# Attention loads on 96 and 80 rows, with edges and repeated rows copied on chip

## The chip, the cores and the metric

The kernel runs on one core of one Trainium2 chip. The metric is the device time of one execution in microseconds, from the timed runs; lower is better. TensorE (PE) multiplies matrices, VectorE (DVE) and ScalarE (ACT) work element by element, GpSimd (POOL) here issues gathers and scatters by index, SyncE (SP) issues the plain DMA transfers, one after another in a fixed order.

## The reference

Sparse attention for 8 batches, 8 heads, 576 positions and 64 numbers per head, followed by a mixture of 8 experts. Heads 0 to 3 look back over the last 32 positions ("local"), heads 4 to 7 over all earlier positions of the same remainder modulo 32 ("strided").

```
scores = scale * q @ k^T
mask_local   = (rel >= 0) & (rel < 32)
mask_strided = (rel >= 0) & (pos_k % 32 == pos_q % 32)
attn = softmax(where(mask, scores, -1e9));  x = attn @ v
logits = x @ w_gate + log1p(exp(x @ w_noise)) * noise
for each token, its two best experts e, with softmax weights w:
    out += w * (relu(x @ w1[e]) @ w2[e])
```

## The kernel before

**Stages.** Attention is done in 32 units: 8 batches x 2 pairs of heads x (strided, local). A unit loads q, k and v of two heads (`loads`), transposes q and k so that the head dimension lies on partitions (`prep`), multiplies scores (`products`), takes exponentials, transposes them and multiplies by v (`item`), and stores the result to a table in DRAM (`finish`). After four units a batch is routed to experts (`route`). The expert stage (`experts`) gathers tokens by index and runs both layers of eight experts. It is by far the longer stage, and starts when the tokens of the first batches are routed.

**A local unit.** `raw` holds four neighbouring positions in each of 128 rows for two heads, 512 positions in all; the last 64 positions of k and q come apart as `kq0`. `raw` is reordered on chip into `ord` (a copy on VectorE or ScalarE, whichever is free earlier), TensorE transposes it in four pieces (L475), one copy empties the result from PSUM into `kT_l` or `qT_l`. `kq0` is transposed at L500 and emptied by two small copies. `v_l` has 96 rows for each block of 64 positions: the 32 rows before the block and the block itself. So each value row that ends a block is loaded twice, and the very first block has a load of its own.

**A strided unit.** `ks` and `qs` hold eight neighbouring positions in each of 72 rows; TensorE transposes them in two halves of four (L485). A query block looks at keys of the same remainder modulo 8; for the first 64 positions a separate operand is kept, which comes from `kq0` again. `v_s` has the values in 72 rows, `v_0` those of the first 64 positions.

**What sets the order.** Every step is a `Piece` with an engine, a duration from a cost function, what it reads and writes, and a rank. `issue_all` goes through all pieces once, at build time, and puts the one that could start earliest by these costs next on its engine; among those within 120 ns the lowest rank goes first. A piece marked "ANY" goes to VectorE or ScalarE. The result is one fixed sequence on each engine. SyncE's loads are costed by their bytes, and 600 ns of SyncE each. On the chip an engine executes its sequence in order and waits for what is not there yet. Buffers are rings: `raw` has two, `ks`, `qs` and `ord` one each, `v_l`, `v_s` and `v_0` two. A load into a ring waits until the last reader of the older content is done.

Names in the profile: L417 is every load of `loads`, L644 every store to the DRAM table `x_dram`; L475, L485 and L500 the transposes of `ord`, of `ks` and `qs`, and of `kq0` (`kq`); L538 the scores; L565 the row maximum `mx`; L569 and L571 exponentials `ex`; L579 the transposes of `ex` into `aT`; L598 the product with v; L262 and L263 copies on ScalarE, L265 and L266 those on VectorE; L1000 and L1064 the expert layers; L871 and L874 loads of expert weights (`wraw`).

Of the kernel before, what the change touches and what calls it, by code (L numbers as in the profile page):

```python
# [9 lines left out]
F32 = mybir.dt.float32  # L10
# [12 lines left out]
def kernel(  # L23
# [24 lines left out]
    G = S // NJ  # L48
    scale = 1.0 / math.sqrt(D)
# [49 lines left out]
    dist = consts.tile([QB, 2, G], I32, name="dist")  # L99
# [27 lines left out]
    TR = E * REG // 128  # L127
# [10 lines left out]
    qT_s = keep.tile([128, NBL, QB], F32, name="qT_s")  # L138
    v_l = [keep.tile([KW, 2, NBL, D + 1], F32, name=f"v_l{i}") for i in range(2)]
    v_s = [keep.tile([G, 2, NJ, D + 1], F32, name=f"v_s{i}") for i in range(2)]  # L140
# [14 lines left out]
    tinit = consts.tile([128, TR // 4, 3], I32, name="tinit")  # L155
# [100 lines left out]
    def dma(fn, nbytes, rank, eng="SP", **kw):  # L256
        return Piece(eng, 600 if eng == "SP" else GAP, fn, rank, lat=nbytes, **kw)
# [151 lines left out]
    def loads(u, rank):  # L409
# [10 lines left out]

        for key, src in (("k", k), ("q", q)):
            if local:

                put(key, R["raw"].new(), [(lambda t: t.rearrange("p h j d -> p h (j d)"), src, base,
                                           [[4 * D, 128], [S * D, 2], [1, 4 * D]], 262144)], True)
            else:
                put(key, R[key + "s"].new(),
                    [(lambda t: t.rearrange("p h j d -> p h (j d)"), src, base,
                      [[NJ * D, G], [S * D, 2], [1, NJ * D]], 294912)], True)

        put("kq0", R["kq0"].new(),
            [(lambda t, r=r: t[r], src, base + (512 * D if local else 0), [[D, QB], [S * D, 2], [1, D]], 65536)
             for r, src in zip(halves, (k, q))], True)
        if local:
            slot = R["v_l"].new()

            parts = [(lambda t: t[STRIDE:, 0, 0, :D], v, base, [[D, QB], [1, D]], 32768),
                     (lambda t: t.rearrange("p h n d -> p (h n) d")[:, 1:, :D], v, base + (QB - STRIDE) * D,
                      [[D, KW], [QB * D, 2 * NBL - 1], [1, D]], 835584)]
            put("v", slot, parts, True)  # L440
        else:
            put("v", R["v_s"].new(),
                [(lambda t, h=h: t[:, h, :, :D], v, base + h * S * D, [[NJ * D, G], [D, NJ], [1, D]], 294912)
                 for h in range(2)], True)
            put("v0", R["v_0"].new(),
                [(lambda t: t[:QB, :, :D], v, base, [[D, QB], [S * D, 2], [1, D]], 65536)], True)
        return res

    def prep(u, L, rank):
# [3 lines left out]
        state = {"k": 0, "q": 0}  # L453

        def evac(which, n, fn, ps, factor):
            slot = kT if which == "k" else qT
            first = state[which] == 0
            state[which] = 1
            Piece("ANY", {"ACT": act(n), "DVE": dve(n)}, fn, rank, read=[ps],
                  **({"alloc": [slot]} if first else {"write": [slot]}))  # L460

        def tile_of(which, c):

            src = L[which]
            ps = Slot()
            if local:

                raw, src = src, R["ord"].new()
                Piece("ANY", {"ACT": act(512) + 30, "DVE": 335}, lambda o: copy(
                    o.e, src.t, raw.t.rearrange("p h j d -> p j h d")), rank, read=[raw], alloc=[src], far=FAR)  # L470

                def tr(o):
                    pv = ps.t.rearrange("r (x j) -> r j x", j=4)
                    for t in range(4):
                        nc.tensor.transpose(pv[:, t, :], src.t[:, t, :, :], ident)  # L475
                Piece("PE", 430, tr, rank, read=[src], psum=ps)
                if which == "k":
                    evac("k", 512, lambda o: copy(o.e, kT.t[:, STRIDE:STRIDE + 512], ps.t), ps, None)
                else:
                    evac("q", 512, lambda o: copy(  # L480
                        o.e, qT.t[:, :8, :], ps.t.rearrange("r (i x) -> r i x", i=8), scale), ps, scale)
            else:
                def tr(o):
                    for jj in range(4):
                        nc.tensor.transpose(ps.t[:, G * jj:G * jj + G], src.t[:, c, 2 * jj:2 * jj + 2, :],  # L485
                                            ident[:G, :G])
                Piece("PE", 260, tr, rank, read=[src], psum=ps)
                if which == "k":
                    evac("k", 288, lambda o: copy(o.e, kT.t[:, 4 * c:4 * c + 4, :], ps.t[:, :4 * G].rearrange(
                        "r (j x) -> r j x", j=4)), ps, None)  # L490
                else:
# [4 lines left out]
        def rest():  # L496
# [5 lines left out]
            def kdst():  # L502
                return kT.t[:, STRIDE + 512:] if local else kT.t[:, NBL - 1, :QB]
# [742 lines left out]
```

## Time and profile before

| | |
|---|---|
| timed runs (3) | 1168.73 us median, 1166.84 to 1169.95 |
| the profiled execution | 1158.95 us, span 1157.1 us |
| busy share of the span | PE 94%, DVE 52%, ACT 35%, POOL 53% |
| granted TensorE clock, mean | 0.965 |
| moved by plain DMA | 98.40 MB in 182,624 packets |
| HBM | 118.86 MB read, 39.39 MB written |

How to read it: the page's strip gives the busy share of 40 equal slices of the span in tenths; "PEclk" is the clock that TensorE was granted, in tenths of full speed. The windows view gives, for any stretch, busy microseconds of each engine with the number of instructions in brackets, the granted clock, the mean busy share of 16 DMA engines and the GB/s moved. The chain of waits is followed back from the last instruction to whatever released each step, so a transfer in it is one that something waited for. A tile's view lists every instruction on it, with durations (shortest/median/longest in ns), and how long an engine sat idle before them and until what. The timeline gives start, duration, engine, line and operation.

### The profile page before, as it was taken

To read this page: it belongs to the slowest core of one execution; us is meant where nothing else is said; L and a number is where in the kernel's file an instruction comes from. 1 tells how busy PE (TensorE), PEld (TensorE's weight loads), DVE (VectorE), ACT (ScalarE), POOL (GpSimd) and SP (SyncE) were. 2 spreads that over 40 slices of the span, in tenths; PEclk is the share of its full clock that TensorE was granted. 3 is DMA by queue.
4 is the path that set the end of the run, shared out by engine and by line. 5 is a ranking of instruction groups with operands and counts; after the bars stand their busy time and mean duration, and the time that the engine had idled before them with its cause. 6 is when DMAs were issued, how large, how long until landed. Compare 5 with 4: busy or idle time off the path is not lost.

```text
span 1157.1 us, 23398 instructions
## 1 busy us (share of the span) xinstructions
PE 1082.1 (94%) x8546; PEld 946.1 (82%) x8546; DVE 603.5 (52%) x1542; ACT 399.9 (35%) x1081; POOL 610.5 (53%) x783
## 2 busy tenths in 40 slices
PE   7888877889899999999999999999999999999994
PEld 6666766668687988888888888898989898888993
DVE  4566776577567435535535536433733553464330
ACT  4555655476354213313313214211411331142220
POOL 1043455456656655655756656555555555656520
PEclk7889998899999999999999999999999999999997
DMA  8877788779987523524524524422632362243210
GB/s 179 199 166 174 183 174 187 178 161 258 257 227 229 172 80 110 164 69 132 153 74 137 156 74 136 143 79 73 175 106 77 103 181 76 64 143 107 74 46 21
DMA packets 207846, 159.03 MB, mean 137 GB/s; under 512 B 90967, under 2 KB 177495, under 8 KB 207712
## 3 DMA queue, kind: packets, MB, share of 16 engines
q1 hardware_dynamic: 182624, 98.40, 33.6%
q0 software_dynamic: 25088, 58.87, 16.7%
q8 instruction: 81, 1.33, 0.5%
q14 instruction: 53, 0.43, 0.1%
HBM read 118.86 MB, written 39.39 MB: 137 GB/s over the span
## 4 chain that ended last, share of the span: by engine, by line
PE 85%; issue 3%; DMA 3%; DVE 3%; ACT 2%; another core or an unknown queue 0%; SPq 0%; POOL 0%; POOLq 0%; DVEq 0%; ACTq 0%
PE bankH L1064 5%; PE bankA L1064 5%; PE bankB L1000 5%; PE bankF L1000 5%; PE bankB L1064 4%; PE bankF L1064 4%; PE bankA L1000 4%; PE bankE L1000 4%; PE bankG L1000 4%; PE bankD L1000 4%; PE bankC L1000 4%; PE bankH L1000 4%; PE bankC L1064 4%; PE bankE L1064 4%; PE bankD L1064 4%; PE bankG L1064 4%
## 5 line engine op out<-in xcount | busy, mean ns | idle before, releaser
L942 POOL DMA_INDIRECT xg<-x_dram,gxx x304 | 308.5, 1015 | 180.1 <-issue 85.5
L806 POOL DMA_INDIRECT tab<-ent,addr x96 | 94.5, 985 | 95.4 <-issue 14.8
L1094 POOL DMA_INDIRECT out_dram<-prev,tabt x80 | 84.9, 1061 | 95.5 <-issue 40.6
L1041 POOL DMA_INDIRECT prev<-out_dram,gix x80 | 78.2, 978 | 65.3 <-issue 22.6
L967 DVE STREAM_TRANSPOSE xr<-xg 128x512 f32<-128x512 f32 x80 | 84.3, 1054 | 35.2 <-DMA xg<-x_dram,gxx 31.8
L971 ACT CAST xhi<-xr 128x512 fp32r<-128x512 f32 x80 | 47.8, 597 | 86.1 <-DVE xr L967 72.4
L877 DVE TENSOR_TENSOR w1lo<-wraw,w1hi 128x512 fp32r<-128x512 f32 x88 | 60.2, 686 | 13.7 <-ACT w1hi L876 5.7
L876 ACT CAST w2hi<-wraw 128x512 fp32r<-128x512 f32 x88 | 52.2, 618 | 42.8 <-DMA wraw<-in_moe_w_dram 23.5
L973 DVE TENSOR_TENSOR xlo<-xr,xhi 128x512 fp32r<-128x512 f32 x80 | 53.1, 664 | 25.2 <-ACT xhi L971 21.0
L877 DVE TENSOR_TENSOR w2lo<-wraw,w2hi 128x512 fp32r<-128x512 f32 x88 | 58.0, 684 | 6.6 <-ACT w2hi L876 4.4
L876 ACT CAST w1hi<-wraw 128x512 fp32r<-128x512 f32 x88 | 54.3, 619 | 15.8 <-DMA wraw<-in_moe_w_dram 11.7
L1019 ACT ACTIVATE hhi<-bankD 128x256 fp32r<-128x256 f32 (+2 forms) x31 | 13.2, 426 | 88.6 <-PE bankD L1000 65.0
L1000 PE MATMUL bankB<-xhi,w1hi 128*128 128x256 f32 (+3 forms) x132 | 40.2, 305 | 1.5 <-ACT hhi L1019 1.3
L1000 PE MATMUL bankE<-xhi,w1hi 128*128 128x256 f32 (+3 forms) x136 | 41.2, 303 | 0.3 <-issue 0.3
L1000 PE MATMUL bankB<-xhi,w1lo 128*128 128x256 f32 (+3 forms) x132 | 40.1, 304 | 0.8 <-issue 0.7
L1000 PE MATMUL bankE<-xhi,w1lo 128*128 128x256 f32 (+3 forms) x136 | 40.5, 298 | 0.0
L1000 PE MATMUL bankF<-xhi,w1lo 128*128 128x256 f32 (+3 forms) x128 | 39.1, 305 | 1.5 <-DVE w1lo L877 1.5
L1000 PE MATMUL bankE<-xlo,w1hi 128*128 128x256 f32 (+3 forms) x136 | 40.2, 296 | 0.0
L1000 PE MATMUL bankB<-xlo,w1hi 128*128 128x256 f32 (+3 forms) x132 | 39.7, 301 | 0.4 <-issue 0.4
L1000 PE MATMUL bankC<-xhi,w1hi 128*128 128x256 f32 (+3 forms) x132 | 39.4, 299 | 0.0
L1000 PE MATMUL bankF<-xhi,w1hi 128*128 128x256 f32 (+3 forms) x128 | 39.1, 305 | 0.3 <-issue 0.3
L1000 PE MATMUL bankC<-xhi,w1lo 128*128 128x256 f32 (+3 forms) x132 | 39.3, 298 | 0.0
(627 smaller groups left out, 3465.9 us busy)
## 6 DMA issues: line engine op xcount, KB each, us to landing
wraw<-in_moe_w_dram SPq DMA_DIRECT2D x176, 256.0 KB
out_dram<-zeros SPq DMA_DIRECT2D x12, 768.0 KB
v_l<-in_v_dram SPq DMA_DIRECT2D x16, 408.0 KB
xg<-x_dram,gxx POOLq DMA_INDIRECT x304
ks<-in_k_dram SPq DMA_DIRECT2D x16, 288.0 KB
qs<-in_q_dram SPq DMA_DIRECT2D x16, 288.0 KB
v_s<-in_v_dram SPq DMA_DIRECT2D x32, 144.0 KB
raw<-in_k_dram SPq DMA_DIRECT2D x16, 256.0 KB
```

The costliest lines, as they stand in the source:

```text
L806: st = nc.gpsimd.indirect_dma_start(out=tab, out_offset=bass.IndirectOffsetOnAxis(ap=s["addr"].t[:, t, kk:kk + 1], axis=0), in_=s["ent"].t ...
L876: Piece("ACT", act(512) + 30, lambda o: nc.scalar.copy(hi.t, raw.t), rank, read=[raw], alloc=[hi], expert=True)
L877: Piece("DVE", dve(512), lambda o: nc.vector.tensor_tensor(lo.t, raw.t, hi.t.bitcast(F32), ALU.subtract), rank, read=[raw, hi], alloc=[lo] ...
L942: dma(lambda o, i=i, g=g, xg=xg: nc.gpsimd.indirect_dma_start(out=xg.t[:, g, :], out_offset=None, in_=x_dram[:4 * known, :], in_offset=bas ...
L967: Piece("DVE", dve(4 * rows), lambda o, xg=xg, xr=xr, ng=ng, rows=rows: nc.vector.transpose(xr.t[:, :, :rows].rearrange("p c (g i) -> p g ...
L971: Piece("ACT", act(4 * rows), lambda o, xr=xr, rows=rows, cols=cols: nc.scalar.copy(xh.t[:, :, cols], xr.t[:, :, :rows]), rank, read=[xr], ...
L973: Piece("DVE", dve(4 * rows), lambda o, xr=xr, rows=rows, cols=cols: nc.vector.tensor_tensor(xl.t[:, :, cols], xr.t[:, :, :rows], xh.t[:, ...
L1000: nc.tensor.matmul(ps.t[:, :width], a.t[:, 128 * d:128 * d + 128], c.t[:, d, :width], start=(m == 0), stop=(m == len(todo) - 1))
L1019: Piece("ACT", act(width) + 30, lambda o: nc.scalar.activation(hh.t[:, :width], ps.t[:, :width], AF.Relu), rank, read=[ps], alloc=[hh], ex ...
L1041: dma(lambda o: nc.gpsimd.indirect_dma_start(out=pv.t[:rows, :], out_offset=None, in_=out[:known, :], in_offset=bass.IndirectOffsetOnAxis( ...
L1064: nc.tensor.matmul(ps.t, HT[n, f][p[0]].t[:, cols], W2[n][f][p[1]].t, start=(m == 0), stop=(m == len(todo) - 1))
L1094: st = nc.gpsimd.indirect_dma_start(out=out[:known, :], out_offset=bass.IndirectOffsetOnAxis(ap=tb.t[:rows, i, 0:1], axis=0), in_=pv.t[:ro ...
```

## The change

Seven edits. (1) `raw` and `ord` hold six neighbours in each of 96 rows, so that all 576 positions come in one load; each is transposed in six pieces of 96 rows, three into each half of `kT_l` or `qT_l`, with one copy out of PSUM for each half. (2) `ks`, `qs` and `v_s` are loaded on 80 rows instead of 72; the last 8 rows are the beginning of the next head and are not used (the very last unit, at the end of the tensor, keeps 72). (3) The loads `kq0` are gone, and with them their transposes. For a local unit the last positions are part of `raw`. (4) For a strided unit the first 64 positions are put together from the transposed tile by eight small copies, each of 64 rows and 32 elements. (5) `qT_s` keeps all 72 columns of a block instead of the last 64. (6) `v_l` loads only the blocks of 64 rows; the 32 rows before each block are copied on chip from the block before (`front`), 32 rows of 17 x 64 elements, once per local unit. The separate load of the first block is gone. (7) The planner books 690 ns of SyncE for a load instead of 600. Besides, `dist`, a temporary of the set-up, shares the memory of `tinit`.

```diff
-            ("raw", [128, 2, 4, D], F32, 2), ("ord", [128, 4, 2, D], F32, 1),
-            ("ks", [G, 2, NJ, D], F32, 1), ("qs", [G, 2, NJ, D], F32, 1),
-            ("kq0", [2 * QB, 2, D], F32, 2),
+            ("raw", [LP, 2, LJ, D], F32, 2), ("ord", [LP, LJ, 2, D], F32, 1),
+            ("ks", [GP, 2, NJ, D], F32, 1), ("qs", [GP, 2, NJ, D], F32, 1),
...
-        return Piece(eng, 600 if eng == "SP" else GAP, fn, rank, lat=nbytes, **kw)
+        return Piece(eng, 690 if eng == "SP" else GAP, fn, rank, lat=nbytes, **kw)
...
-        put("kq0", R["kq0"].new(),
-            [(lambda t, r=r: t[r], src, base + (512 * D if local else 0), [[D, QB], [S * D, 2], [1, D]], 65536)
-             for r, src in zip(halves, (k, q))], True)
         if local:
             slot = R["v_l"].new()
-            parts = [(lambda t: t[STRIDE:, 0, 0, :D], v, base, [[D, QB], [1, D]], 32768),
-                     (lambda t: t.rearrange("p h n d -> p (h n) d")[:, 1:, :D], v, base + (QB - STRIDE) * D,
-                      [[D, KW], [QB * D, 2 * NBL - 1], [1, D]], 835584)]
-            put("v", slot, parts, True)
+            put("v", slot, [(lambda t: t[STRIDE:].rearrange("p h n d -> p (h n) d")[:, :, :D], v, base,
+                             [[D, QB], [QB * D, 2 * NBL], [1, D]], 589824)], True)
+
+            def front(o):
+                vv = slot.t.rearrange("p h n d -> p (h n) d")
+                copy(o.e, vv[:STRIDE, 1:, :D], vv[QB:, :2 * NBL - 1, :D])
+            Piece("ANY", {"ACT": act(64 * (2 * NBL - 1)), "DVE": 640}, front, rank, read=[slot], write=[slot])
...
+                        for j in range(LJ // 2):
+                            nc.tensor.transpose(pv[:, j, :], src.t[:, LJ // 2 * c + j, :, :], ident[:LP, :LP])
...
+        if not local:
+            for _, slot, _ in tens:
+                for c, r in enumerate(halves):
+                    for odd, ro in enumerate(halves):
+                        Piece("ANY", {"ACT": act(32), "DVE": dve(32)}, lambda o, slot=slot, c=c, r=r, odd=odd, ro=ro: copy(
+                            o.e, slot.t[r, NBL - 1, :QB].rearrange("r (x j g) -> r j x g", j=NJ // 2, g=2)[:, :, :, odd],
+                            slot.t[ro, 4 * c:4 * c + 4, :QB // NJ]), rank, read=[slot], write=[slot])
```

Here G is 72, GP 80, LP 96, LJ 6, NJ 8, QB 64, STRIDE 32, NBL 9 and D 64. Since every piece is placed anew, the sequence on every engine is another one; two places are shown in the prediction.

More of the change, by code (lines that the diff above doesn't have):

```diff
@@ L48 @@
     G = S // NJ
+    GP = G + 8
+    LP, LJ = S // 6, 6
     scale = 1.0 / math.sqrt(D)
@@ L419, in put @@
             res[key] = slot
+        rows = GP if units[u][:2] != (B - 1, NP - 1) else G
         for key, src in (("k", k), ("q", q)):
```

97 lines of the change are left out of this document (37 added, 60 removed).

## Prediction

> **What bounds the kernel now.** First the page's strip: 40 slices of 28.9 us.
>
> ```profile
> PE   7888877889899999999999999999999999999994
> PEclk7889998899999999999999999999999999999997
> DMA  8877788779987523524524524422632362243210
> ```
>
> The left quarter is unlike the rest: TensorE has holes and a reduced clock, the DMA engines are full. The windows view, cut at the stages, says the same in numbers (us busy of PE, PEld, DVE, ACT, POOL; granted clock, DMA share, GB/s).
>
> ```profile
> 40.00:290.00 250.00, 210.60 (x3260) 171.57 (x3249) 165.81 (x691) 144.17 (x513) 111.75 (x208) 0.92 0.80 186
> 350.00:1100.00 750.00, 744.34 (x4253) 666.93 (x4253) 366.37 (x642) 201.62 (x426) 448.70 (x489) 1.00 0.40 119
> ```
>
> From 350 us on TensorE has no room (744 of 750 us at full clock): the experts, which the change leaves alone. Whatever the change is worth is made in attention, up to about 290 us, where TensorE idles 39 us of 250, and what is won there moves the end by as much. Next the chain of waits over the first 300 us: the row that groups it by line, and its pieces on loads of strided k tiles (start, us, what).
>
> ```profile
> by line: DMA ks<-in_k_dram 9.4%; issue 8.4%; PE bankG L579 2.3%; PE bankC L598 2.1%; PE bankB L579 2.0%; PE bankD L598 1.9%; PE bankH L1064 1.9%; ACT ex L569 1.9%; PE bankE L485 1.7%; PE bankH L598 1.6%; PE bankG L598 1.6%; PE bankD L670 1.
> ...
> 43.53 4.14 DMA ks<-in_k_dram
> ...
> 126.65 4.22 DMA ks<-in_k_dram
> ...
> 162.28 4.06 DMA ks<-in_k_dram
> ...
> 175.33 6.19 DMA ks<-in_k_dram
> ...
> 196.19 5.67 DMA ks<-in_k_dram
> ```
>
> No other single item is as large: five times after the start the chain runs through a whole `ks` load, 24.3 us together. How much of that TensorE really idled stands in the view of that tile, and what follows an idle stretch in the windows.
>
> ```profile
>   DMA ks<-in_k_dram: 10.2, 5
> ```
> ```profile
> 44.00:48.00 4.00, 0.19 (x2) 0.22 (x3) 0.00 (x0) 0.42 (x1) 0.00 (x0) 0.79 0.71 166
> 48.00:52.00 4.00, 4.00 (x35) 2.96 (x37) 1.35 (x5) 0.79 (x2) 0.00 (x0) 0.50 0.97 219
> 52.00:56.00 4.00, 4.00 (x86) 2.77 (x81) 1.04 (x3) 1.09 (x4) 0.00 (x0) 0.86 1.08 267
> ...
> 184.00:188.00 4.00, 4.00 (x53) 2.75 (x54) 1.73 (x5) 0.80 (x2) 2.23 (x5) 0.72 0.58 152
> ...
> 204.00:208.00 4.00, 4.00 (x29) 3.46 (x29) 2.29 (x4) 1.20 (x3) 0.00 (x0) 0.50 0.71 160
> ```
>
> TensorE waited 10.2 us for `ks`, in five places, and after three of them its clock was cut: 4 us x (0.50 + 0.14 + 0.28 + 0.50) = 5.7 us of full-clock work lost. So the late `ks` costs about 15.9 us.
>
> **Why ks is late.** The tile has one buffer, and SyncE issues all loads and stores in one order. SyncE's own rows (issue time min/median/max in ns), and its timeline ahead of the load at 175.33:
>
> ```profile
> L417 SPq DMA_DIRECT2D kq<-in_k_dram x32: 600/632/1362, 1.7 to 257.2; - x32
> L417 SPq DMA_DIRECT2D kq<-in_q_dram x32: 595/632/2074, 4.2 to 261.2; - x32
> L417 SPq DMA_DIRECT2D v_l<-in_v_dram x32: 319/574/1843, 9.6 to 257.9; - x32
> ```
> ```profile
> 170.28 0.62 SPq L417 DMA_DIRECT2D kq<-in_k_dram  x1
> 171.03 1.12 SPq L644 DMA_DIRECT2D x_dram<-xo  x2
> 172.19 0.59 SPq L417 DMA_DIRECT2D v_l<-in_v_dram  x1
> 173.15 2.07 SPq L417 DMA_DIRECT2D kq<-in_q_dram  x1
> 175.33 0.50 SPq L417 DMA_DIRECT2D ks<-in_k_dram  x1
> ```
>
> An issue takes about 0.6 us whatever it carries: a 16 KB half of `kq` as much as a 288 KB `ks`.
>
> **The change part by part.** *Issues removed.* Each of 32 units loses two `kq` loads, each of 16 local ones the small first-rows load of `v_l`: 64 x 0.632 = 40.4 us and at least 16 x 0.319 = 5.1 us, 45.5 us of SyncE's queue in 300. SyncE at the same place, ahead of the `ks` of the twelfth strided unit (the load at 175.33), before the change (`kq`: first or last positions; `v_l`: local values; `xo`: finished attention):
>
> ```order
> L707 DMA noise<-in_moe_noise_dram 96x6x8
> L417 DMA v_l_123<-in_v_dram 64x64
> L417 DMA kq_2535<-in_k_dram 64x2x64
> L644 DMA x_dram<-xo_130 128x4x128
> L644 DMA x_dram<-xo_130 64x128
> L417 DMA v_l_123<-in_v_dram 96x17x64
> L417 DMA kq_2535<-in_q_dram 64x2x64
> L417 DMA ks<-in_k_dram 72x2x512
> ```
>
> and in the changed kernel:
>
> ```order
> L695 DMA noise<-in_moe_noise_dram 96x6x8
> L421 DMA raw<-in_q_dram 96x2x384
> L421 DMA v_l_123<-in_v_dram 64x18x64
> L632 DMA x_dram<-xo_131 128x4x128
> L632 DMA x_dram<-xo_131 64x128
> L421 DMA raw<-in_k_dram 96x2x384
> L421 DMA ks<-in_k_dram 80x2x512
> ```
>
> Three issues are gone from ahead of `ks`, 0.62 + 0.59 + 2.07 = 3.3 us in the trace, and the planner has put the `raw` loads into part of the room. A mean wait was 10.2 / 5 = 2.0 us, so most should vanish, but some of those queues were held by zero fills and weights that stay. I take three quarters of 15.9: **-11.9 us**. The ends are 0 (the load is still late) and 24.3 + 5.7 = -30 us (the chain's pieces vanish whole). With `kq` goes TensorE's own wait for it, the rows of that tile:
>
> ```profile
>   issue: 0.8, 1
>   DMA kq<-in_q_dram: 0.7, 1
> ```
>
> **-1.5 us**; between 0 and that, since the eight copies below could be waited for instead.
>
> *Transfers.* Per pair of units the load shapes sum to 1,960 KB in 4,288 runs before (`v_l` 1,696, `kq` 512, `raw` 512, `ks` and `qs` 288, `v_s` 1,152, `v` 128) and 1,856 KB in 3,264 after. What that is worth alone is the first rival; in the sum it stays inside the term above.
>
> *TensorE.* 32 `kq` and 128 local transposes of 128 columns become 192 of 96.
>
> ```profile
> 172.07 0.60 PE L475 MATMUL bankG<-ident,ord 128*128 128x128 f32 x4
> ...
> 172.76 0.27 PE L500 MATMUL bankC<-ident,kq 128*128 128x128 f32 x1
> ```
>
> Four take 0.60 and the last alone 0.27, so one every 0.11 us: 17.6 us go; 192 cost 15.8 (by columns) to 21.1 (the same each). I take the lower half: **0**, ends -1.8 and +3.5.
>
> *Copies added to VectorE and ScalarE.* The nearest rows: smallest copy-like operations from on-chip memory to itself on either engine, the old reorder, and ScalarE's spacing.
>
> ```profile
> L746 ACT ACTIVATE wt<-wt x8: 207/208/208, 58.8 to 307.6; 96x6 f32<-96x6 f32 x8
> ```
> ```profile
> L615 DVE RECIPROCAL rs<-rs x32: 122/126/129, 18.5 to 295.9; 64x2 f32<-64x2 f32 x32
> ```
> ```profile
> L265 DVE COPY ord<-raw x18: 408/410/481, 19.3 to 214.9; 128x512 f32<-128x512 f32 x18
> ...
> L262 ACT COPY ord<-raw x14: 610/618/656, 14.8 to 267.4; 128x512 f32<-128x512 f32 x14
> ```
> ```profile
> 175.40 0.21 ACT L262 COPY kT_s<-bankC 128x64 f32<-128x64 f32 x1
> 175.51 0.23 ACT L263 ACTIVATE qT_s<-bankC 128x64 f32<-128x64 f32 x1
> 175.62 0.59 ACT L262 COPY kT_l<-bankG 128x512 f32<-128x512 f32 x1
> ```
>
> The order gives 57 of the 128 small copies (64 rows x 32 elements) to VectorE, 71 to ScalarE: 57 x 0.126 + 71 x 0.208 = 22 us. ScalarE's slope is (0.59 - 0.21) / 448 = 0.85 ns an element, so a front copy (32 rows x 1,088) takes 0.618 + 576 x 0.00085 = 1.11 us, 13 of them 14.4; VectorE's three at 0.410 x 1088 / 512 = 0.87 add 2.6. The reorder of 768 elements instead of 512 costs 16 x 0.205 + 16 x 0.218 = 6.8. Emptying PSUM stays level for local units (two of 288 for one of 512 and one of 64), and the strided ones lose 32 small evacuations, -6.7. Together some +39 us over two engines that were busy 166 and 144 of 250 us: these gaps cover it where nobody waits. It is waited for ahead of the scores of a strided unit. ScalarE between the exponentials of the unit at 172.87 us and those of the next, before (`ex`: exponentials, `kT_s` and `qT_s`: strided operands):
>
> ```order
> L571 ACTIVATE ex<-bankD,mx 64x96
> L571 ACTIVATE ex<-bankE,mx 64x96
> L262 COPY kT_s<-bankC 128x64
> L263 ACTIVATE qT_s<-bankC 128x64
> L262 COPY kT_l<-bankG 128x512
> L262 COPY xT<-bankA 128x64
> L262 COPY aT<-bankB 96x512
> L262 COPY aT<-bankE 96x128
> L569 ACTIVATE ex<-bankC,mx 128x72 x4
> ```
>
> and now:
>
> ```order
> L559 ACTIVATE ex<-bankC,mx 64x96
> L559 ACTIVATE ex<-bankE,mx 64x96
> L267 COPY kT_s<-kT_s 64x4x8
> L267 COPY qT_s<-qT_s 64x4x8
> L267 COPY kT_l<-bankA 128x96x3
> L267 COPY qT_s<-qT_s 64x4x8
> L267 COPY kT_s<-kT_s 64x4x8
> L267 COPY qT_s<-qT_s 64x4x8
> L267 COPY xT<-bankB 128x64
> L267 COPY qT_s<-qT_s 64x4x8
> L267 COPY aT<-bankC 96x128
> L557 ACTIVATE ex<-bankE,mx 128x72 x4
> ```
>
> Two evacuations became six copies, and the `aT`, `xT` and the scores behind them wait in line. Split over both engines, four copies follow each other at 0.11 us (ScalarE's spacing) to 0.208 (no overlap): 0.44 to 0.83 us a strided unit, 0 to 13.3 us for 16. I take 0.44 for five late units, 2.2, and as much for all others: **+4.4 us**. A front copy also waits for its load, with ScalarE's queue behind it; the reorder has that kind of wait already and its view shows 1.1 us of it in all, so I add nothing.
>
> Here the Trainium skill speaks against the change: "VectorE: DVE Perf Modes", section "The TRN2 errata", says that an operation from SBUF pays a fixed cost for each instruction, so that many small ones are dear; it gives 58 cycles plus the elements at 0.96 GHz for VectorE. By that a 32-element copy takes 94 ns where the row has 126, the 57 copies 5.4 us instead of 7.2, and the covered work +37 instead of +39; the path, counted by ScalarE's row, would stay.
>
> Sum: -11.9 - 1.5 + 0 + 4.4 = **-9.0 us**. The profiled execution took 1158.95 us (span 1157.1), so 1149.9 for its like. It ran 9.8 us under the median of the timed runs, 1168.73; the same step gives **1159.7** there.
>
> **Rivals.** *1, the transfers themselves are the bound of attention* (DMA share 0.80; 1.08 in the crowded window above).
>
> ```profile
> q1 hardware_dynamic: 182624, 98.40, 33.6%
> ```
>
> 0.336 x 16 x 1157.1 / 182,624 = 34 ns a packet; 1,024 fewer a pair x 16 pairs x 34 ns over 16 engines = -35 us: 1133.8. For it: the share, and loads of 4 to 6 us. Against: TensorE, not DMA, carries most of the chain. Chance 0.20. A rule of the Trainium skill would make it more ("DMA: Bandwidth & Descriptors", section "Why a DMA increments its semaphore by 16 and not by 1": a transfer uses the largest number of engines up to 16 that divides its slowest dimension, so 72 rows use 12 and 80 rows 16). By it 1,440 runs a pair lay on 12 engines, and their relief adds 1,440 x 34 ns x (1/12 - 1/16) x 16 = 16 us, an estimate (1117.4); no row shows one DMA engine by itself, and of the 0.20 I give this 0.05.
>
> *2, `ks` stays late:* with one buffer the load cannot start before the previous tile's last transpose, and a load still takes 4 us. The copies eat what is left: 0, 1168.7. For it: 39 us of holes have many owners, issue 8.4% among them. Chance 0.16.
>
> *3, slower: the small copies before the strided scores.* If TensorE reaches the scores sooner than the last copy, each of 16 units pays 0.83 us, +13.3, and with `ks` no earlier 1182.0. It decides from the point at which the `ks` transposes come less than a microsecond ahead of the scores; in the trace of before that is so in about five units of 16 (+4), hence the weight on half the price. Chance 0.16.
>
> **How the numbers follow.** Forecast 0.48, rivals 0.20, 0.16, 0.16. Faster by over 0.3% (3.5 us, about what a measurement tells from no change): 0.68; the same 0.16; slower 0.16. The likeliest case alone runs from -20 to -3.5. For eight in ten the range goes down to rival 1's price and up into the near part of rival 3 (+5.3, about the five late units at 0.83 and a little): 1134 to 1174. Outside stay the steeper form of rival 1 and the far half of rival 3, some 0.15 with what I have not thought of.
>
> **What would show it.** Right: no `ks` load of over 2 us in the chain after the start, TensorE's wait for `ks` under 4 us, fewer windows at clock 0.5, SyncE with 80 issues fewer, 350 to 1100 us unchanged but earlier. Wrong: `ks` pieces as long as before, TensorE's scores waiting for `kT_s` or `qT_s` copies, ScalarE waiting for `v_l` loads, or small copies far over 0.21 us.

## The result and the profile after

The changed kernel took 1176.71 us in the median of 4 runs (1173.68 to 1179.07), the kernel before 1169.3 beside it (4 runs, 1166.84 to 1169.95): a ratio of 1.0066, with a 95% interval of 1.0037 to 1.0095. It is slower; the forecast was 1159.7. The profiled execution took 1173.68 us, its span 1172.0 against 1157.1 before. That execution of before was 8 us shorter than the shortest timed one, so the two profiles lie twice as far apart as the medians. Here and below, an execution at a lower clock that took over 1.5% more than the kernel's fastest is left out of ratios and means (one of after, one of e6, both on stopping chips, explained below). First its page's strip, then the windows by stage, with columns as before:

```profile
PE   7978887889997999999999999999999999999994
...
PEclk7997978798998999999999999999999999999997
DMA  9897767677887223443534524422532362243210
```
```profile
40.00:290.00 250.00, 212.42 (x3159) 172.67 (x3148) 174.77 (x721) 171.05 (x550) 105.29 (x196) 0.87 0.77 184
350.00:1100.00 750.00, 734.41 (x4183) 657.68 (x4183) 355.78 (x622) 196.53 (x417) 447.97 (x488) 0.99 0.39 117
```

TensorE's idle time in the first row is hardly less (250 - 212.42 = 37.6 us, before 39.4), and its granted clock fell from 0.92 to 0.87: 250 x 0.08 = 20 us of full-clock work lost before, 250 x 0.13 = 32.5 now. ScalarE is 27 us busier, VectorE 9. Attention is where it was lost: its last product with v ends at 294.4 us before and at 309.7 after. The windows up to there, before and after:

```profile
0.00:294.40 294.40, 248.67 (x3754) 202.14 (x3754) 191.01 (x785) 167.85 (x590) 118.50 (x237) 0.91 0.81 186
```
```profile
0.00:309.70 309.70, 265.73 (x3798) 216.75 (x3798) 213.14 (x854) 205.62 (x654) 120.13 (x239) 0.86 0.79 187
```

Idle time is 45.7 and 44.0 us, clock lost 26 and 43: the second difference is about the whole 15 us. From there to TensorE's end both take the same (845.4 and 844.9 us). The forecast's "350 to 1100 us unchanged" does not hold within that stretch: TensorE idles 15.6 us in it, before 5.7, and 8.2 of them are one hole at 364 us, which after has on the quick chip too (the rows of the two):

```profile
PE bankB L988 <- issue: 8.2, 1, 8.2
```
```profile
PE bankB L988 <- ACT xhi L959: 8.3, 1, 8.3
```

The row that names nobody ("issue") is thus not proof that nothing was waited for.

The loads did what was forecast. The chain of waits over the first 300 us, by line, and TensorE's wait in the view of `ks`:

```profile
by line: issue 5.6%; ACT ex L557 3.1%; PE bankF L586 2.7%; PE bankE L586 2.7%; DVE mx L553 2.6%; PE bankA L567 2.1%; DMA v_l<-in_v_dram 2.1%; PE bankG L586 2.1%; PE bankB L567 1.9%; PE bankG L658 1.9%; PE bankB L526 1.9%; PE bankC L567 1.9%
...
6.53 4.74 DMA ks<-in_k_dram
...
79.63 6.28 DMA v_l<-in_v_dram
```
```profile
  DMA ks<-in_k_dram: 2.2, 2
```

`ks`, at 9.4% the largest row before, is gone but for the start, and TensorE waited 2.2 us for it in place of 10.2. So 8 us of one wait went, and the idle time fell by 1.8. What came instead is in the waits of TensorE from 40 to 300 us (line waited for, us in total, times, longest):

```profile
PE bankH L658 <- DVE xo L610: 2.9, 1, 2.9
...
PE bankG L658 <- DVE xo L607: 2.3, 3, 1.6
...
PE bankC L658 <- DVE xo L607: 1.6, 1, 1.6
...
PE bankD L658 <- DVE xo L610: 1.3, 2, 0.9
```

These are transposes of the finished attention `xo` that stand ahead of other work in TensorE's order; all waits for `xo` together are 11.4 us, before 4.1. The longest ends at 164.7 us; the windows around it show what follows a hole:

```profile
160.00:164.00 4.00, 1.61 (x9) 0.89 (x7) 1.71 (x24) 1.81 (x8) 1.25 (x2) 1.00 0.45 106
164.00:168.00 4.00, 3.31 (x31) 2.95 (x31) 3.43 (x19) 2.92 (x10) 2.23 (x5) 0.58 0.99 255
168.00:172.00 4.00, 3.90 (x67) 3.18 (x65) 2.57 (x6) 3.90 (x12) 1.70 (x5) 0.50 0.74 188
172.00:176.00 4.00, 3.53 (x22) 3.04 (x22) 2.22 (x9) 2.73 (x11) 1.64 (x4) 0.50 0.29 67
176.00:180.00 4.00, 4.00 (x47) 3.12 (x49) 3.01 (x8) 2.14 (x5) 2.59 (x3) 0.50 0.61 162
```

TensorE stands for 2.4 of 4 us, and then works at half clock for 17 us.

### The profile page after: what moved, and what is told of

It reads as the page before. It is cut to its first block, busy times and chain, and to the rows that moved or that the text cites. A ratio compares the mean times of both kernels' runs of the same rounds, so it can differ in the third digit from the quotient of the medians.

```text
span 1172.0 us, 23426 instructions
## 1 busy us (share of the span) xinstructions
PE 1093.4 (93%) x8578; PEld 956.7 (82%) x8578; DVE 618.8 (53%) x1601; ACT 430.5 (37%) x1134; POOL 612.0 (52%) x783
## 4 chain that ended last, share of the span: by engine, by line
PE 86%; DVE 5%; issue 2%; ACT 2%; DMA 2%; another core or an unknown queue 0%; POOL 0%; SPq 0%; POOLq 0%; DVEq 0%; ACTq 0%
PE bankF L1052 5%; PE bankB L1052 5%; PE bankG L1052 5%; PE bankE L988 5%; PE bankA L988 5%; PE bankH L988 4%; PE bankC L988 4%; PE bankD L988 4%; PE bankG L988 4%; PE bankA L1052 4%; PE bankF L988 4%; PE bankB L988 4%; PE bankD L1052 4%; PE bankE L1052 4%; PE bankC L1052 4%; PE bankH L1052 4%
## 5 line engine op out<-in xcount | busy, mean ns | idle before, releaser
L930 POOL DMA_INDIRECT xg<-x_dram,gxx x304 | 312.2, 1027 | 187.6 <-issue 90.9
L961 DVE TENSOR_TENSOR xlo<-xr,xhi 128x512 fp32r<-128x512 f32 x80 | 53.1, 664 | 25.5 <-ACT xhi L959 23.9
L1007 ACT ACTIVATE hhi<-bankA 128x256 fp32r<-128x256 f32 (+2 forms) x33 | 14.0, 425 | 94.3 <-PE bankA L988 79.3
L988 PE MATMUL bankF<-xhi,w1hi 128*128 128x256 f32 (+3 forms) x128 | 39.4, 308 | 2.5 <-ACT xhi L959 2.5
L1007 ACT ACTIVATE hhi<-bankC 128x256 fp32r<-128x256 f32 (+2 forms) x31 | 13.2, 426 | 76.3 <-PE bankC L988 64.3
L988 PE MATMUL bankA<-xhi,w1hi 128*128 128x256 f32 (+3 forms) x132 | 40.3, 305 | 0.4 <-issue 0.4
L988 PE MATMUL bankA<-xhi,w1lo 128*128 128x256 f32 (+3 forms) x132 | 39.9, 302 | 0.0
L988 PE MATMUL bankA<-xlo,w1hi 128*128 128x256 f32 (+3 forms) x132 | 39.7, 301 | 0.0
L988 PE MATMUL bankF<-xlo,w1hi 128*128 128x256 f32 (+3 forms) x128 | 38.8, 303 | 0.3 <-DVE xlo L961 0.3
```

What stands on the lines that cost most here:

```text
L930: dma(lambda o, i=i, g=g, xg=xg: nc.gpsimd.indirect_dma_start(out=xg.t[:, g, :], out_offset=None, in_=x_dram[:4 * known, :], in_offset=bas ...
L961: Piece("DVE", dve(4 * rows), lambda o, xr=xr, rows=rows, cols=cols: nc.vector.tensor_tensor(xl.t[:, :, cols], xr.t[:, :, :rows], xh.t[:, ...
L988: nc.tensor.matmul(ps.t[:, :width], a.t[:, 128 * d:128 * d + 128], c.t[:, d, :width], start=(m == 0), stop=(m == len(todo) - 1))
L1007: Piece("ACT", act(width) + 30, lambda o: nc.scalar.activation(hh.t[:, :width], ps.t[:, :width], AF.Relu), rank, read=[ps], alloc=[hh], ex ...
```

## The experiments

**Two kinds of chip.** The runs fell on several chips, and these are of two kinds. On three (1, 2 and 11) before took 1143 to 1144 us; I call them *quick*. On two (6 and 12) it took 1164, near the 1169 of the result; I call them *stopping*, for a reason shown below. Kernels are compared only through their ratio to before on the same chip. For every profile a sum of two things is given: idle time of TensorE from 40 to 290 us (250 less its busy time) and clock lost there (250 x (1 - granted clock)). Time in which TensorE stands at half clock counts in both: 7 us of before on the quick chip, at most 3 in the other rows.

| kernel | chip | ratio to before (95%) | idle + clock lost, us |
|---|---|---|---|
| before | quick | 1 | 40.6 + 25.0 |
| after | quick | 0.9828 (0.9790 to 0.9866) | 18.1 + 25.0 |
| e6, no copies | quick | 0.9720 (0.9695 to 0.9745) | 19.5 + 10.0 |
| e10, before without kq0 loads | quick | 0.9804 (0.9769 to 0.9839) | 18.3 + 7.5 |
| before | stopping | 1 | 39.4 + 20.0 |
| after | stopping | 1.0066 and 1.0047 (1.0013 to 1.0080) | 37.6 + 32.5; 35.8 + 30.0 |
| e6b, no copies | stopping | 1.0022 (0.9984 to 1.0061) | 29.2 + 42.5 |

**e1, e2, e3: one part undone, or both** (quick; before 1143.2 us).

```diff
# shortened
# e1: strided units load the first 64 positions again and transpose them
+            put("kq0", R["kq0"].new(), ...)
-            eight copies of 64 rows x 32 elements
# e2: v_l loaded as in before
-            Piece("ANY", ..., front, rank, read=[slot], write=[slot])
+            put("v", slot, parts, True)
# e3: both
```

> After, but the strided units load the first 64 positions of q and k again (32 loads more than after) and turn them with a TensorE transpose and two evacuations, so the eight small copies of kT_s and qT_s are gone. Theory A (the copies that the change adds to VectorE and ScalarE lie on the path to the scores, with about 0.6 of their time): 28 us of small copies less, some 6 us of evacuations back, so -13 us, and about +5 us for the loads and transposes that come back: 1169 us, 6 to 10 us under after. Theory B (the cost is in the split local evacuations and the longer ord copies): no more than 2 us under after, or above it, since loads come back: 1176 to 1181. Theory C (no work of the change costs much, the planner's new order is unlucky and any other order moves it by some us): no forecast of the sign, within 8 us of after.

> After, but v of the local units is loaded as in before (all 17 blocks of 96 rows and the first rows by an own load; 16 loads and 8 MB more), and the copy of the repeated rows of v_l is gone. Theory A: 13 x 1.09 + 3 x 0.75 = 16.4 us of ScalarE and VectorE less, of which 0.6 lay on the path, -10 us, and the loads that come back +2 us: 1168 to 1170. Theory B: within 2 us of after. Theory C: within 8 us of after, no sign.

> After, with both undone: the first positions of q and k of the strided units loaded again, v of the local units loaded as in before; what stays of the change is six neighbours on 96 rows in the local units (with their split evacuations and 768-element ord copies), 80 rows in the strided units and the planner's 690 ns. Theory A: the two gains add, 1160 to 1163. Theory B: as after, 1176 to 1180. Theory C: the steps don't add.

Measured: e1 0.9835 (0.9802 to 0.9868), 1124.39 us; e2 0.9843 (0.9811 to 0.9875), 1124.94; e3 0.9961 (0.9935 to 0.9987), 1139.1. The first surprise was not in the differences but in the level, 18 us under before. With after itself on such a chip (below, 0.9828), undoing either part alone changes nothing that can be measured, and undoing both costs 15 us. Theory A wanted gains and got none. Theory B (as after) fits e1 and e2, and not e3. So copies and the loads that they replace look like an even trade one by one, and worth having together; but each run has an order of its own, so this is not shown.

**e4: only the 80 rows** (quick).

```diff
-            ("ks", [G, 2, NJ, D], F32, 1), ("qs", [G, 2, NJ, D], F32, 1),
+            ("ks", [GP, 2, NJ, D], F32, 1), ("qs", [GP, 2, NJ, D], F32, 1),
```

> Before, with the one thing changed that ks, qs and v_s are loaded on 80 rows instead of 72 (same number of loads, 11% more bytes in these). Theory A says nothing of it by itself. If the late ks loads of before were a matter of the number of loads (as the prediction had it), 1168 to 1171, the ks waits in the middle of attention stay. If they were a matter of how few of the 16 DMA engines a 72-row load reaches, the ks waits shrink and it is 8 to 12 us under before: 1157 to 1161.

Measured: 1.0052 (1.0030 to 1.0074), 1150.6 us. The wait for `ks` was shorter than in before on a quick chip (its row stands further below), 17.4 us, and other loads were later. Rows of the views of `ks` and of the groups by form, 40 to 290 us:

```profile
  DMA ks<-in_k_dram: 17.4, 5
```
```profile
L264 ACT COPY ord<-raw 128x512 f32<-128x512 f32 x15 | 9.5, 631 | 11.1 <-DMA raw<-in_k_dram 10.9
```

The rows alone bring nothing: ScalarE now waits 10.9 us for `raw`, in before on a quick chip 0.9.

**r2_after, r2_before, r3_after: both kernels on the chips of the experiments.** No edit.

> The kernel after, unchanged, beside the kernel before, to have both on the same chip as the experiments of this call, since the kernel before took 1143 us on the chip of the first four and 1169 us on the first one. If the ratio belongs to the kernels: 1.004 to 1.010 of before. If it is a matter of how fast the chip's transfers are (the steps of before that wait for loads shrink on a faster chip, the added copies don't): a ratio over 1.01. If the elementwise theory A holds and e1 and e2 gained because they drop copies, after lies 6 to 12 us over both of them.

> The kernel before, unchanged, for its profile on this chip. If the difference between the chips lies in the transfers: a higher GB/s in the window 40 to 290 us than the 186 of the first profile, shorter ks waits, and the same durations of matmuls and copies.

> The kernel after once more, unchanged, beside before, on the chip of this call. Theory D (attention has a load side and a compute side; the change takes from the first and gives to the second, so its sign depends on which side a chip makes longer): where before takes about 1143 us, after takes 1120 to 1130; where before takes about 1169, after takes 1172 to 1180. Theory A (the copies lie on the path everywhere): a ratio over 1.00 on either.

Measured: on a quick chip after takes 1124.75 us, 0.9828 (0.9790 to 0.9866); on a stopping one 1168.94, 1.0047 (1.0013 to 1.0080). So the sign belongs to the pair of kernel and chip. The slower result repeats on a second stopping chip; after itself ran on one quick chip only. None of the three expectations of r2_after came true (1.004 to 1.010, over 1.01, 6 to 12 us over e1 and e2). Windows and `ks` view of before on the quick chip, and then of after there:

```profile
40.00:290.00 250.00, 209.37 (x3332) 174.92 (x3331) 172.41 (x708) 147.76 (x523) 119.27 (x216) 0.90 0.84 197
```
```profile
  DMA ks<-in_k_dram: 31.2, 7
```
```profile
40.00:290.00 250.00, 231.87 (x3476) 191.99 (x3475) 197.20 (x795) 186.48 (x599) 124.23 (x223) 0.90 0.93 218
```
```profile
  DMA ks<-in_k_dram: 2.2, 4
```

On the quick chip before waits 31.2 us for `ks`, three times as long as in the first profile; after takes that away, and the idle time falls by 22.5 us at the same granted clock. Some of that is paid back: before stood idle in part of its half-clock time, and after works in nearly all of it, so the work lost at half clock rises from 18 to 25 us. The chip's transfers don't explain the difference of the chips by themselves: GB/s is higher than in the first profile (197 and 186), the waits for `ks` are longer, not shorter, and a reorder copy takes the same 410 and 618 ns. The span falls by 13.1 in these two executions (1143.9 to 1130.8, of which the second is one of after's longest), and 18.6 in the medians.

One profile is one execution, and 23 executions of before on one stopping chip range over 17 us. But every timed execution has its span and mean clock on record. Clock lost is the span x (1 - clock), the rest is the span less that; means in us:

| kernel | chip | executions | span | clock lost | rest |
|---|---|---|---|---|---|
| before | quick (1) | 11 | 1142.1 | 43.0 | 1099.1 |
| after | quick (1) | 6 | 1123.9 | 37.3 | 1086.6 |
| before | stopping (12) | 29 | 1161.5 | 42.4 | 1119.1 |
| after | stopping (12) | 11 | 1165.9 | 55.5 | 1110.3 |

On the stopping chip the rest falls by 8.8 us, and the clock takes 13.1; on the quick chip both fall. The kernel before loses the same to the clock on both kinds: what a stopping chip costs it lies in the rest, 20 us.

What the stopping chip does otherwise is best seen in one group of 16 value matmuls (line 586), whose inputs are all there when the first starts. TensorE's timeline of after on the chip of the result, and on the quick chip (start, us, what, count, idle before):

```profile
187.61 0.33 PE L586 MATMUL bankA<-v_l,aT 96*64 96x65 f32 x3
188.54 0.29 PE L586 MATMUL bankA<-v_l,aT 96*64 96x65 f32 x2 [0.60 <-issue]
189.27 0.22 PE L586 MATMUL bankA<-v_l,aT 96*64 96x65 f32 x1 [0.44 <-issue]
189.99 0.51 PE L586 MATMUL bankA<-v_l,aT 96*64 96x65 f32 x10 [0.50 <-issue]
```
```profile
175.92 0.69 PE L586 MATMUL bankA<-v_l,aT 96*64 96x65 f32 x16
```

The same instructions take 2.9 us with three stops, and 0.69 with none. Stops also come between 420 and 1110 us, where no wait is shown; the rows of that window in the result's profile are

```profile
PE bankC L988 <- issue: 2.7, 5, 0.9
PE bankA L1052 <- issue: 0.9, 2, 0.7
PE bankA L988 <- issue: 0.4, 1, 0.4
PE bankD L988 <- issue: 0.3, 1, 0.3
```

while the quick chip's answer for the same window has no row at all. The stops are no mark of after: from 40 to 290 us the "issue" rows sum to 14.1 us in 31 waits in before on the chip of the result, and to 9.9 in 18 in after; on the quick chip to 0.5 and 0.8.

**e5: the planner's 600 ns** (both times quick).

```diff
-        return Piece(eng, 690 if eng == "SP" else GAP, fn, rank, lat=nbytes, **kw)
+        return Piece(eng, 600 if eng == "SP" else GAP, fn, rank, lat=nbytes, **kw)
```

> After, with the one number of the planner back, 600 ns of SyncE for an issue in place of 690, which changes no instruction but their order. Theory A: within 3 us of after. Theory C (an unlucky order): moves by more than 5 us, either way.

> After with the planner's 600 ns, as e5. Where before takes 1143: 0.972 to 0.977 again. Where it takes 1164: by theory G no better than after, 1.000 to 1.007, as e9 (1.0061) which has the 600 ns too.

Measured: 0.9745 (0.9718 to 0.9772) and 0.9726 (0.9697 to 0.9754), that is 9 to 12 us under after, from the same work in another order (on balance four of the "ANY" pieces moved from VectorE to ScalarE). The row of the second shows both parts of the sum lower than in after (17.2 + 10.0):

```profile
40.00:290.00 250.00, 232.81 (x3574) 195.12 (x3573) 206.91 (x826) 197.15 (x620) 137.47 (x236) 0.96 0.94 228
```

Theory C is right so far: the order is worth half as much as the whole change (18.6 us) or more. This is the best complete kernel that was run; it was not run on a stopping chip.

**e6: the copies left out.**

```diff
-            Piece("ANY", {"ACT": act(64 * (2 * NBL - 1)), "DVE": 640}, front, ...)
-                        Piece("ANY", {"ACT": act(32), "DVE": dve(32)}, ...)
```

> After, with the eight small copies of the strided units and the front copy of v_l left out (so the strided scores of the first 64 positions and the first 32 rows of the later v_l blocks are zeros: this part of the computation is missing), all loads as in after: what the change would be if its copies cost nothing. Theory A: 28 + 16 us of VectorE and ScalarE less than after, of which 0.6 were on the path: 20 to 27 us under after. Theory B: no more than 3 us under after. Theory C (the order alone): within 8 us of after, either way.

> After without its small copies and front copies (the strided scores of the first 64 positions and the first 32 rows of the later v_l blocks are left out), as in e6, in case this chip is of the other kind. Theory D (little to win on the loads there): where before takes about 1165 us, 1150 to 1158, a ratio of 0.988 to 0.994 in place of 0.972. Theory E (as much to win on the loads, but dear copies): 1130 to 1140, a ratio under 0.98. Where before takes 1143 again: 0.970 to 0.975.

Measured: on the quick chip 0.9720, 1112.39 us, so all of the change but its copies is worth -31.0 us there, and the copies cost +12.4 in the order of after. The order is part of that price: e5, with all the copies, took 1115.47 us on the same chip, 3.1 over e6. On the stopping chip 1.0022 (0.9984 to 1.0061), 1171.09 us: not faster than before, and not to be told from after. The windows of the same program on the quick and on the stopping chip:

```profile
40.00:290.00 250.00, 230.54 (x3572) 193.80 (x3571) 197.31 (x776) 171.84 (x549) 136.09 (x236) 0.96 0.98 230
```
```profile
40.00:290.00 250.00, 220.81 (x3118) 181.15 (x3116) 167.22 (x647) 148.94 (x479) 103.78 (x188) 0.83 0.75 182
```

This pair decides against theories A, D and E. Between the profiles of before and e6 on the quick chip the last product with v moves from 286.1 to 270.2 us, 15.9 of the 33.2 us by which the spans differ; the rest is won behind it, where 29 matmuls of the experts fewer are left to do and TensorE waits less. With no copies and no `ks` to wait for, the stopping chip's TensorE is idle 10 us less than in before and loses 22.5 us more to the clock.

**e7 and e8: more copies** (all four times stopping).

```diff
# e7: before, with the copies added as work that is not needed
+            Piece("ANY", {"ACT": act(32), "DVE": dve(32)}, ...)   # eight a strided unit
+            Piece("ANY", {"ACT": act(64 * (2 * NBL - 1)), "DVE": 640}, front, ...)
# e8: after, every copy twice
-            for _, slot, _ in tens:
+            for _, slot, _ in tens + tens:
```

> Before, with all its loads, plus the small copies and the front copy of after as work that is not needed (eight copies of 64 rows x 32 elements into the last block of kT_s for each strided unit, which write there what kq0 put there; the front copy of v_l over rows that were loaded). Theory D: before waits for loads, so 44 us of copies cost it 0 to 6 us. Theory A: +20 to +27 us, as many as e6 should have gained against after.

> Before plus the copies of after as work that is not needed, as in e7, which cost 19.4 us where before took 1164. Theory D: where before takes 1143, its loads are late and cover the copies: +0 to +8 us. Theory E: no more than half of the 19.4 us either. If the copies cost the same on every chip: +15 to +24 us, and then D and E are both wrong on what covers them.

> After, with every small copy and every front copy done twice. Leaving them out gained 12.4 us (e6). Theory D, compute side now the longer one: the second dose costs as much as the first or more, +12 to +27 us over after. If the first dose was mostly covered and 12.4 us is a matter of the order: within 5 us of after.

> After with each copy done twice, as in e8, which was 6.5 us faster than after where before took 1164. Where before takes 1143: if the copies have a price of their own there (12.4 us for the first dose), +10 to +25 us over after, a ratio of 0.99 to 1.005; if the planner's order is all that counts, any ratio within 0.7% of the 0.983 of after.

Measured: e7 1.0165 (1.0123 to 1.0206) and 1.0175 (1.0134 to 1.0217), +19 and +21 us; e8 0.9996 (0.9968 to 1.0023) and 1.0013 (0.9983 to 1.0042), which is 6 us *under* after on the first of these chips. So on a stopping chip the same copies cost 20 us in one order, nothing in a second (e6b), and a double dose less than nothing in a third. No price per copy fits all of it. The profile of e7 shows one wait of 1.9 us for `ks` in the whole run, with all of before's loads still there: on a stopping chip that wait can go without one load less. Of e7's 19 us 13 are clock lost (55.5 us in the mean of its executions, before 42.4). On a quick chip e7 and e8 were not run.

**e9: four merged copies and 600 ns** (stopping).

```diff
-    kT_s = keep.tile([128, NBL, G], F32, name="kT_s")
-    qT_s = keep.tile([128, NBL, G], F32, name="qT_s")
+    kq_s = keep.tile([128, 2, NBL, G], F32, name="kq_s")
+    kT_s, qT_s = kq_s[:, 0], kq_s[:, 1]
...
-        return Piece(eng, 690 if eng == "SP" else GAP, fn, rank, lat=nbytes, **kw)
+        return Piece(eng, 600 if eng == "SP" else GAP, fn, rank, lat=nbytes, **kw)
...
-                        Piece("ANY", {"ACT": act(32), "DVE": dve(32)}, ...)
+                    Piece("ANY", {"ACT": act(64), "DVE": dve(64)}, ...)
```

> After, with kT_s and qT_s as halves of one tile, so that one copy moves the positions of both and a strided unit has four copies of 64 elements in place of eight of 32, and with the planner's 600 ns back. Against after with 600 ns (1115.5 where before took 1143.4): fixed costs of four copies saved, 4 x 0.15 x 16 = 10 us of engine time, of which at the measured rate (12.4 us of the path for 44 us of copies) 3 us lie on the path: a ratio to before of 0.970 to 0.975. It would cost instead (0.975 to 0.985) if waiting for both evacuations before the first copy outweighs that.

Measured: 1.0061 (1.0033 to 1.0089). The forecast was meant for a quick chip. Its row has the largest sum of all, 40.3 + 40.0:

```profile
40.00:290.00 250.00, 209.72 (x3050) 171.96 (x3050) 166.06 (x683) 165.51 (x510) 105.44 (x193) 0.84 0.71 175
```

**e10: the load term alone** (quick).

```diff
+        if u > 1:
+            res["kq0"] = LL[u - 2]["kq0"]
+        else:
             put("kq0", R["kq0"].new(), ...)
```

> Before with the kq0 loads left out after the first two units (60 issues of SyncE fewer; the later units turn the old rows again, so their first or last 64 positions are wrong; nothing else is changed): the load term of the prediction by itself, 60 of its 80 issues. Load theory, as on the fast kind of chip: 0.975 to 0.988 of before on either kind. Theory G (on the kind where before takes 1164, the time that the loads free comes back as holes and lost clock of TensorE): 0.995 to 1.005 there, 0.975 to 0.988 where before takes 1143.

Measured: 0.9804 (0.9769 to 0.9839), 1120.49 us. Sixty kq0 loads less, with no other work changed, though with a new order, are worth -23.5 us on a quick chip, about 0.4 us an issue; TensorE's wait for `ks` is 7.8 us in its profile, in before there 31.2. The half of theory G on the other kind could not be tried.

**e11: transposes of xo planned later** (quick).

```diff
-            Piece("PE", 110 if c else 430, tr, rank, read=[xo], psum=ps)
+            Piece("PE", 110 if c else 430, tr, rank, read=[xo], psum=ps, late=1500)
```

> After with one number more in the planner: the transposes of xo count as ready 1.5 us later than before, so that other work of TensorE is put ahead of them; same instructions, another order. TensorE waited some 11 us for xo in after where before takes 1164 to 1169, and 3 us where it takes 1143. Theory G: on the slow kind 8 to 20 us under after (the waits and the half-clock windows behind them), a ratio of 0.988 to 0.998; on the fast kind within 4 us of after (0.980 to 0.986). If holes move elsewhere as fast as they are closed: within 4 us of after on either.

Measured: 0.9899 (0.9862 to 0.9935), 1132.61 us, 8 us over after and outside what was expected. Its sum is 17.6 + 20.0, lower than after's, and its last product with v ends 7 us earlier (270.1, after 277.4). What it loses comes behind attention, in one hole of TensorE ahead of an expert's first layer, twice as long as in after (8.3 us):

```profile
PE bankH L988 <- ACT xhi L959: 16.7, 1, 16.7
```

So time won in attention was lost again behind it, and the sum, which ends at 290 us, does not see that: it orders kernels only roughly. Whether it helps where `xo` was waited for is open.

## Why the prediction was wrong

**The step that failed** is "I take three quarters of 15.9: -11.9 us", with its reason that the late `ks` costs its wait and, behind it, the clock. The wait went as forecast (10.2 to 2.2 us). The clock did not come with it. The sign that was to show the step right, fewer windows at clock 0.5, is the one that came out wrong: clock lost in 40 to 290 us rose from 20.0 to 32.5 us, while other waits took the place of the first (`xo` 4.1 to 11.4). The idle time saved is 1.8 us and the clock lost extra 12.5; the profiled span is 14.9 us longer. The executions on record say the same without the choice of one profile: apart from the clock a stopping chip saves 8.8 us, more than the forecast's -4.7 without its clock part (3/4 x 5.7 = 4.3 of the 9.0), and loses 13.1 to the clock. e6b, with fewer loads and no copies, has the same two terms (-8.7 and +11.5 beside before on its chip) and is no faster than before.

The forecast took the clock to come back with the wait that is saved. It did not: up to 300 us half clock begins 9 times in the profile of before and 14 times in that of after, and lasts 51 and 85 us in all, at nearly the same idle time (45 and 42 us).

**On quick chips the same step was too small.** Before waited 31.2 us for `ks` there; the loads' side gained 31.0 us (e6, with its own order), against -13.4 for both load terms and -30 as the far end of the first. The direction is that of the forecast, in the wait, in the clock (-5.7 us over the executions) and in the time; that 0.9828 lies inside its range (1134 to 1174 of 1168.73 is 0.970 to 1.0045) is partly luck, since the range was worked out from a chip of the other kind. The profile of before came from a stopping chip, and 10.2 us was what such a chip leaves to win.

**The price of the copies** (+4.4, ends 0 and 13.3) was 12.4 us on a quick chip in the order of after, 3.1 in that of e5, and not measurable on a stopping one (e6b against after). So the forecast of it is neither confirmed nor refuted. The durations of the small copies were too low. Rows of the `kT_s` and `v_l` views and of `ord` in after (ns min/median/max):

```profile
L267 ACT COPY kT_s<-kT_s x33: 235/247/251, 6.8 to 275.7; 64x32 f32<-64x32 f32 x33
...
L270 DVE COPY kT_s<-kT_s x31: 178/192/331, 8.4 to 258.0; 64x32 f32<-64x32 f32 x31
```
```profile
L267 ACT COPY v_l<-v_l x13: 1086/1097/1102, 17.0 to 269.7; 32x1088 f32<-32x1088 f32 x13
```
```profile
L267 ACT COPY ord<-raw x16: 808/832/846, 13.7 to 213.6; 96x768 f32<-96x768 f32 x16
...
L270 DVE COPY ord<-raw x16: 525/549/557, 19.4 to 281.6; 96x768 f32<-96x768 f32 x16
```

A small copy takes 192 ns on VectorE where I had 126 from a reciprocal, and 247 on ScalarE where I had 208: 57 x 0.192 + 71 x 0.247 = 28.5 us in place of 22. The front copy on ScalarE (1.11 forecast) and the reorder there (+0.218 forecast, +0.214 measured) were right; on VectorE the reorder grew by 0.139 instead of 0.205. By the row of the Trainium skill that I weighed ("VectorE: DVE Perf Modes", section "The TRN2 errata") a small copy would take 94 ns on VectorE; the trace has twice that. I had overlooked that the same section says that this row under-predicts and gives a measured fixed term of about 150 cycles. By that the copy takes (150 + 32) / 0.96 = 190 ns, an estimate, and the trace's 192 ns agrees.

**kq0 and TensorE's transposes** (-1.5 and 0): nothing in the runs speaks against them; they were not taken apart. A `kq` load carries 32 KB (64 x 2 x 64 numbers of four bytes), not the 16 KB that the prediction names; the sum does not use it.

**Rival 1**, transfers as the bound, had -35 us; quick chips show -31.0 without the copies and -23.5 from 60 small loads (e10). So the number was near; its reason, packets over engines, was not tested apart from the issues. Its steeper form, the rule of the Trainium skill that 80 rows reach 16 engines and 72 only 12 ("DMA: Bandwidth & Descriptors", section "Why a DMA increments its semaphore by 16 and not by 1"), promised 16 us by my estimate: e4, which has that alone, is 7 us slower. **Rival 2** (0) named the right doubt, that the holes have many owners, with the wrong reason: `ks` was not late. **Rival 3** had the sign and not the mechanism: TensorE's strided scores waited only 0.8 us for `kT_s` and `qT_s` copies in after, and leaving the copies out does not help measurably there.

**What stays open.** What the stops of TensorE are, and why the clock falls more in after than in before on a stopping chip and not on a quick one. More stops in after are not the reason, since before has more of them (14.1 us against 9.9). The waits for `xo` and the clock lost grew together. On one stopping chip e8 and e9, with other copies and so another order, lie 6.5 us under after and 1.8 over it, so the loss may be the order alone, and no second order of after's own instructions was run there. That fewer loads are worth nothing by themselves on a stopping chip is only argued, from e6b; e10 ran on a quick one.

## What to carry to other kernels

A wait that is taken away pays only if the engine behind it can use the time: add up its idle time and its lost clock before and after, not the one wait. When a planner sets the order, any edit also draws a new order, here worth 9 to 12 us (e5); run a second order of the same instructions before an edit is praised or blamed. Split the time of every execution into clock lost and the rest: here that split, not the profile of one execution, shows what each side did. And run before and after on more than one chip when the effect is about 1%: here its sign turned with the chip.

## What was not expected of the hardware

- The same program took about 2 to 5% longer on some chips than on others (e6: 1112 and 1171 us; before: 1143 and 1164), with equal durations of single copies. TensorE's stops without a wait that the profile shows, in places such as the middle of the 16 matmuls above, went with the longer time. From 300 to 1100 us VectorE and ScalarE too stood longer with no releaser shown (before: 72 and 58 us on the chip of the result, 2 and 0 on the quick one); some of this may be waits that the profile could not name, as the hole of 8.2 us was.
- In the clock records of before, after and e6, on both kinds of chip, all stretches at half clock ahead of the last one last 3.4 us or a multiple of it (up to 23.9), and up to 300 us each of them follows 3.4 us in which TensorE idled at least 0.76 us (up to 3.41). The converse holds mostly: in the result's profile of after 13 of 60 such periods at full clock had over 1 us idle, and 11 of the 13 were followed by half clock, as were 3 of the other 47; in before it was 9 of 13 and none of 58.
